# Turning y with a DMA transpose from the sixth pair of chunks on, in a fused gated-recurrence and MLP kernel

## The chip, the cores and the metric

The kernel runs on one core of one Trainium2 chip. Five engines run side by side, each with its own list of instructions: PE (TensorE, matrix products), ACT (ScalarE), DVE (VectorE), POOL (GpSimd) and SP (SyncE, which here only starts transfers). The metric is the device time of one execution in microseconds. Three runs of the kernel before gave 177.77, 177.81 and 180.62 us; the median is 177.81.

## The reference

First a recurrence with decay, for 4 sequences of 768 tokens, 8 heads of 48 dimensions; then an MLP with squared ReLU on every token:

```python
for t in range(S):                       # S = 768, state is D x D per head, D = 48
    state = alpha[:, :, t, :, None] * state + np.einsum('bhd,bhe->bhde', k[:, :, t], v[:, :, t])
    y[:, :, t] = np.einsum('bhd,bhde->bhe', q[:, :, t], state)
x = y.transpose(0, 2, 1, 3).reshape(3072, 384)
out = np.square(np.maximum(x @ w_in, 0)) @ w_out      # w_in 384 x 2048, w_out 2048 x 384
```

Inputs and output are float32; the products run in bfloat16 and sum in float32.

## The kernel before

**Tiling.** A chunk is 128 tokens and a pair is two chunks, 256 tokens of one sequence. There are 12 pairs (`g` from 0 to 11), three to a sequence; the state passes from chunk to chunk inside a sequence. The sixth pair is `g` = 5. One partition holds two neighbouring tokens (an even and an odd one), so that a tile of 128 partitions and 2 x 384 columns is a pair.

**Stages of a pair.**
- `loads`: four transfers of 384 KB on SP's queue (alpha, k, q, v), into one of four buffers RAW.
- `decay`: DVE and ACT turn alpha into running products, with a small product on PE (`sums`, L502 and L504; L541 and L546 in the first two pairs). k and q are scaled by them into QKS (L523, or L555).
- `turned`: QKS is transposed into QKT, with dimensions on partitions. The first three pairs do it on PE (L606, L574); from the fourth on (`TURN` = 3) one DMA transpose on SP's queue does it (L586, 16 blocks of 128x128, 512 KB).
- `scores`: q times k inside a chunk on PE (L634), masked by DVE into PMB (L644).
- `carry`: k times v on PE (L663); DVE and POOL make the next states of it in SBF (L681, L683).
- `mixed`: y = scores times v plus q times the state before (L702). It is computed turned, features on partitions and tokens along the columns: 48 products of 64 rows, 64 weights and 128 columns from PMB and VBF, and 24 (12 in the first pair of a sequence) from QKT and SBF. The last half of the 24 waits until the others have left PE, since it works crosswise on the same rows and banks. ACT copies the two results (L739) into XT, which is as the next stage reads it.
- `up`: eight units a pair on PE (L756, 12 products of 128x128 weights and 256 columns each); ACT takes the ReLU (L760), DVE the square (L762). Two PSUM banks, psH, hold the results in turn.
- `down`: for each chunk four parts on PE (L780, 4 products of 384 columns each), a copy by ACT (L787) and a store of 192 KB (L789). `last_down` (L800) does the last chunk in two halves.

`scores`, `carry` and `mixed` use the array as four tiles of 64x64; the others use it whole. The planner marks these operations with `form=64`.

**What sets the order.** `add` records every operation with what it reads and writes, an estimated length (`work`) and a due time (`at`, in chunks). `Program.order` plays the whole kernel through on those estimates, engine by engine: of the operations that are ready it takes the one with the earliest due time, keeps PE in one form where the due times allow it, and models SP's and POOL's transfers as queues. The order that results is written into the program; waits on semaphores are then placed where two engines meet (`plan`). The due times come from offsets by stage: EARLY for the first two pairs, MID for the third, OFF for the others (L811 to L813). `fill` puts products on zeros (`busy`, L769) into PE's idle times before the first `down`, to keep its clock up.

**Weights.** w_in and w_out come on POOL's queue in eight pieces of 786 KB (L446, L449), the first of them issued after alpha of the second pair has landed. The loads of the third pair wait for the sixth piece, `wout1` (`OPENS`). Loads on SP keep their order among themselves (`behind`).

Of the kernel before, what the change touches and what calls it, by code (L numbers as in the profile page):

```python
# [15 lines left out]
class Op:  # L16


    def __init__(self, n, eng, fn, work, at, dma=None, nbytes=0, rate=0.0):
# [7 lines left out]
        self.form = None  # L27


class Program:  # L30
# [4 lines left out]
    RESERVE, LATE = 200, 1200.0  # L35
    AHEAD = 4
    BEGIN = {"SP": 1200.0, "POOL": 2200.0}
    LANDING = {"SP": 900.0, "POOL": 1400.0}
    PAIR, ROWS, TURN = 320.0, 390.0, 135.0
    PACKET = {PAIR: 384.0, TURN: 256.0}  # L40
    LONG = 1792.0
    HOLD = 2500.0
    SWITCH, STICK = 95.0, 1.0

# [7 lines left out]
    def add(self, eng, fn, work, at, reads=(), writes=(), dma=None, nbytes=0, rate=0.0, behind=None, form=None,  # L52
            drain=None):
# [25 lines left out]
        op.form = form  # L79
# [3 lines left out]
    def order(self):  # L83
# [26 lines left out]
        def transfer(limit):  # L110

            while now[0] < limit:
# [20 lines left out]
                if queue[first][0][1] <= 1e-3:  # L133
                    op = queue[first].pop(0)[2]
                    op.landed = op.landed0 = end + self.LANDING[first]
                    if op.at > -2 and op.rate == self.PAIR:
                        op.landed += self.LATE
                    if first == "SP":
                        landed.append(op.landed0)
# [10 lines left out]
        form = None  # L150
        while left:
# [38 lines left out]
            if e == "PE":  # L190
                if op.form != form:
                    op.work += self.SWITCH
                form = op.form
            free[e] = t + op.work
# [21 lines left out]
        self.programs = programs  # L216

# [85 lines left out]
def bass_gla_recurrent__then__act_relu_squared_kernel(  # L303
# [31 lines left out]
    NS, NU, NAC, NRO = 5, 3, 3, 2  # L335
    NGT, NRR, NOS = 3, 4, 8
# [17 lines left out]
    XT = sb("xt", [128, KT, G * TW], BF16)  # L354
# [72 lines left out]
    WH = 4  # L427
    FIRST = 2
    TURN = 3
    SELF = 12  # L430


    RUNS = [(1, 3, 8)]
    OPENS = {2: 5}
    pieces = [(w, n) for w in ("in", "out") for n in range(WH)]
    last_weight, last_load = [None], [None]

    def weights(at, run):
        x0 = sum(r[2] for r in RUNS[:run])
        w0, j0, n0 = RUNS[run]  # L440
        for x in range(x0, x0 + n0):
            which, i = pieces[x]
            gate = raw(w0, j0) if x == x0 else []
            if which == "in":
                w = DFF // WH
                fn = lambda g, i=i, w=w: g.dma_start(WIN[:, :, i * w:(i + 1) * w], win_src[:, :, i * w:(i + 1) * w])  # L446
            else:
                w = FT // WH
                fn = lambda g, i=i, w=w: g.dma_start(WOUT[:, i * w:(i + 1) * w, :], wout_src[:, i * w:(i + 1) * w, :])  # L449
            last_weight[0] = add("POOL", fn, 770, at, reads=gate, writes=[("w" + which, i)], dma=f"w{which}{i}",  # L450
                                 nbytes=DM * DFF * 4 // WH, rate=(305.0, 305.0, 370.0, 370.0, 395.0)[min(x, 4)],
# [12 lines left out]
    def loads(g, at):  # L464
        b, t0, r = g // NW, (g % NW) * TW, g % NRAW
        for j, src in ((3, alpha), (0, k), (1, q), (2, v)):
            s = src[b, :, t0:t0 + TW, :].rearrange("h (p i) d -> p h (i d)", i=2)
            dst = RAW[:, r, j, :].rearrange("p (h e) -> p h e", h=H)
            gate = [("w" + pieces[OPENS[g]][0], pieces[OPENS[g]][1])] if g in OPENS and j == 3 else []
            cuts = (0, 1) if g == 0 and j == 3 else (None,)  # L470
            for X in cuts:
# [5 lines left out]
                                   nbytes=TW * HD * 4 // len(cuts), rate=pr.PAIR, behind=last_load[0])  # L477
# [9 lines left out]
    def decay(g, at):  # L487
# [19 lines left out]
        add("PE", sums, 265, at + 0.02, reads=lab + ["hinc"], writes=[key])  # L507
# [388 lines left out]
```

## Time and profile before

| | |
|---|---|
| median of 3 runs | 177.81 us |
| profiled execution, its own time | 177.77 us |
| its span, first to last instruction | 175.8 us |
| PE busy | 168.7 us (96%), 2648 products |
| DVE busy | 116.5 us (66%) |
| ACT busy | 116.2 us (66%) |
| SP's queue | 28.32 MB, 65.0% of the DMA engines' time |
| POOL's queue (weights) | 3.15 MB by its packets, 11.6% |

The span is 1.97 us shorter than the execution's own time. All times in this document are counted from the start of the span. PE is busy in nearly all of it, but some of that work is fill: 22 products on zeros, 7.5 us, all in the first 27 us. The granted clock of PE is 9 tenths or more in all 40 slices. A product's own duration in a row is its way through the array; products overlap, so that what one costs is the distance between two starts. The start times of the timeline rows are therefore subtracted from each other where a cost is wanted.

### The profile page before, as it was taken

What the parts mean: (1) busy time and instruction counts of PE and PEld (TensorE: products, weight loads), DVE (VectorE), ACT (ScalarE), POOL (GpSimd) and SP (SyncE); (2) the same over time, 40 slices, a digit from 0 to 9 for tenths busy, and PEclk for the clock granted to TensorE, in tenths of its full rate; (3) what the DMA queues carried; (4) which work ended last, traced back from release to release, by engine and by line L of the source; (5) the groups of instructions that cost most, each with busy time, mean ns of one, the idle gap of its engine ahead of it and who ended that gap; (6) DMA issues with size and microseconds to landing.
All of it is one profiled execution on the core that took longest, in us unless ns stands there. A gap on an engine that the chain in (4) does not pass through costs nothing.

```text
span 175.8 us, 6062 instructions
## 1 busy us (share of the span) xinstructions
PE 168.7 (96%) x2648; PEld 123.7 (70%) x2648; DVE 116.5 (66%) x251; ACT 116.2 (66%) x235; POOL 18.6 (11%) x35
## 2 busy tenths in 40 slices
PE   7889979999999999999999999999999999999994
PEld 2556658775677777777777776777777777767763
DVE  7895925589979597887965966946836733621410
ACT  4774555695885888879788869747546544645631
POOL 4089300001100201001002001001002000000000
PEclk9999999999999999999999999999999999999999
DMA  5999999999999999999999998901901701101112
GB/s 131 303 300 179 197 203 244 278 318 301 239 248 277 250 261 246 307 180 306 243 235 312 258 265 239 141 28 50 164 4 48 164 4 48 45 4 45 45 45 90
DMA packets 75993, 31.83 MB, mean 181 GB/s; under 512 B 69184, under 2 KB 75968, under 8 KB 75968
## 3 DMA queue, kind: packets, MB, share of 16 engines
q1 hardware_dynamic: 72256, 28.32, 65.0%
q0 software_dynamic: 3712, 3.15, 11.6%
q8 instruction: 20, 0.33, 0.7%
q14 instruction: 5, 0.04, 0.1%
HBM read 25.17 MB, written 4.72 MB: 170 GB/s over the span
## 4 chain that ended last, share of the span: by engine, by line
PE 87%; DVE 3%; ACT 3%; DMA 3%; issue 2%; SPq 1%
PE psH L756 35%; PE psO L780 34%; PE psG L702 8%; PE psG L634 4%; DMA raw<-in_q_dram 3%; DVE pm L644 2%; PE psG L663 2%; ACT xt L739 2%; PE psO L800 2%; PE psG L502 1%; DVE qks L555 1%; ACT rr L760 1%; SPq L474 1%; PE psG L574 1%; DVE ust L681 1%
## 5 line engine op out<-in xcount | busy, mean ns | idle before, releaser
L760 ACT ACTIVATE rr<-psH 128x512 bf16<-128x512 f32 x96 | 56.9, 599 | 35.5 <-PE psH L756 34.6
L756 PE MATMUL psH<-xt,win 128*128 128x256 bf16 x576 | 74.3, 273 | 0.5 <-ACT xt L739 0.4
L780 PE MATMUL psO<-wout,gt 128*128 128x384 bf16 x368 | 71.2, 326 | 0.0
L756 PEld LDWEIGHTS psH<-xt,win 128*128 128x128 bf16 x576 | 54.8, 98 | 13.9 <-ACT xt L739 0.8
L762 DVE TENSOR_TENSOR gt<-rr 128x512 bf16<-128x512 bf16 x96 | 39.8, 425 | 36.7 <-ACT rr L760 36.3
L780 PEld LDWEIGHTS psO<-wout,gt 128*128 128x128 bf16 x368 | 34.5, 98 | 17.2
L644 DVE TENSOR_TENSOR pm<-psG,mask 128x512 bf16<-128x512 f32 x48 | 30.9, 684 | 1.2 <-PE psG L634 1.2
L523 DVE TENSOR_TENSOR qks<-raw,asb 128x768 bf16<-128x768 f32 x20 | 18.4, 956 | 8.1 <-ACT asb L512 8.1
L683 POOL TENSOR_TENSOR sbf<-ust,acp 128x192 bf16<-128x192 f32 x16 | 8.8, 551 | 119.1 <-DVE ust L681 119.1
L739 ACT ACTIVATE xt<-psG 128x384 bf16<-128x384 f32 x24 | 12.6, 596 | 6.6 <-PE psG L702 6.6
L787 ACT ACTIVATE osb<-psO 128x384 f32<-128x384 f32 x23 | 11.4, 494 | 5.2 <-PE psO L780 4.8
L702 PEld LDWEIGHTS psG<-pm,vbf 64*64 64x64 bf16 x576 | 8.4, 107 | 3.7 <-issue 1.8
L702 PE MATMUL psG<-pm,vbf 64*64 64x128 bf16 x576 | 10.4, 218 | 0.6 <-DVE qks L555 0.3
L493 DVE TENSOR_TENSOR raw<-raw 128x384 f32<-128x384 f32 x20 | 10.6, 551 | 0.0
L512 ACT ACTIVATE asb<-psG 128x384 bf16<-128x384 f32 x20 | 9.9, 495 | 1.1 <-PE psG L504 0.8
L702 PE MATMUL psG<-qkt,sbf 64*64 64x128 bf16 x240 | 8.6, 220 | 1.0 <-issue 1.0
L634 PEld LDWEIGHTS psG<-qkt 64*64 64x64 bf16 x384 | 5.8, 106 | 4.3 <-issue 2.4
L634 PE MATMUL psG<-qkt 64*64 64x128 bf16 x384 | 8.1, 219 | 0.6 <-ACT qkt L617 0.4
L769 PE MATMUL psO<-warm 128*128 128x512 bf16 x22 | 7.5, 463 | 1.1 <-DVE warm L391 1.1
L485 ACT ACTIVATE vbf<-raw 128x768 bf16<-128x768 f32 x10 | 8.4, 841 | 0.0
L681 DVE TENSOR_TENSOR ust<-psG,sbf 128x192 f32<-128x192 f32 x15 | 5.3, 355 | 2.6 <-POOL sbf L683 1.9
L498 ACT ACTIVATE lab<-raw 128x384 bf16<-128x384 f32 x10 | 5.2, 520 | 2.2 <-DVE raw L493 2.2
(65 smaller groups left out, 99.5 us busy)
## 6 DMA issues: line engine op xcount, KB each, us to landing
raw<-in_k_dram SPq DMA_DIRECT2D x12, 384.0 KB, 5.0
raw<-in_q_dram SPq DMA_DIRECT2D x12, 384.0 KB, 5.6
raw<-in_v_dram SPq DMA_DIRECT2D x12, 384.0 KB, 5.4
out_dram<-osb SPq DMA_DIRECT2D x23, 192.0 KB, 2.0
raw<-in_alpha_dram SPq DMA_DIRECT2D x11, 384.0 KB, 4.5
win<-in_moe_w_in_dram POOLq DMA_DIRECT2D x4, 384.0 KB, 7.9
wout<-in_moe_w_out_dram POOLq DMA_DIRECT2D x4, 384.0 KB, 12.4
raw<-in_alpha_dram SPq DMA_DIRECT2D x2, 192.0 KB, 2.8
```

Source lines behind the costliest of these rows:

```text
L493: add("DVE", lambda e: e.tensor_tensor(dst, a0, a1, ALU.mult), 470, at_, reads=reads, writes=writes)
L512: add("ACT", lambda act, z=z: act.activation(ASB[a][:, z, 0, :], ps[:, 0:HD], AF.Exp, scale=2.0 * z - 1.0), 372, at + 0.04 + 0.02 * z, rea ...
L523: add("DVE", lambda dve, z=z, decays=decays: dve.tensor_tensor(QKS[x][:, z, :, :, 0:D], both(r, z), decays, ALU.mult), 870, at + 0.05 + 0. ...
L634: last = pe.matmul(banks[i, j // 2][0][64 * c:64 * c + 64, col:col + 128].rearrange("p (a b) -> p a b", a=2), QKT[t][64 * i:64 * i + 64, 0 ...
L644: add("DVE", lambda dve, i=i, X=X, ps=ps: dve.tensor_tensor(PMB[m][:, i, 2 * X:2 * X + 2].rearrange("p j n s -> p j (n s)"), ps[:].rearran ...
L702: last = pe.matmul(o, lhsT, rhs, start=(c, n % 2) not in begun, stop=True, skip_group_check=True)
L739: add("ACT", lambda act, ps=ps, base=base: act.activation(XT[:, :, base:base + C].rearrange("f k (p i) -> f k i p", i=2), ps[:, 0:HD].rear ...
L756: last = pe.matmul(ps[:, f * TW:(f + 1) * TW], WIN[:, kt, fj * 128:(fj + 1) * 128], XT[:, kt, g * TW:(g + 1) * TW], start=(kt == 0), stop= ...
L760: add("ACT", lambda act: act.activation(RR[r][:], ps[:], AF.Relu), 480, at, reads=[key], writes=[key, ("rr", r)])
L762: add("DVE", lambda dve: dve.tensor_tensor(gt[:, 2 * u:2 * u + 2, :], rr, rr, ALU.mult), 340, at, reads=[("rr", r)], writes=[("gt", g % NG ...
L780: last = pe.matmul(ps[:, 0:DM], GT[g % NGT][:, fj, tt * 128:(tt + 1) * 128], WOUT[:, fj, :], start=(fj == 0), stop=(fj == FT - 1))
L787: add("ACT", lambda act: act.activation(OSB[o][:], ps[:, 0:DM], AF.Copy), 372, at, reads=[key], writes=[key, ("osb", o)])
```

## The change

From the sixth pair on (`BACK` = 5), `mixed_back` takes the place of `mixed`. It computes y with tokens on partitions: 64 products of 48 columns from PMB and VBF, and 32 (16 in the first pair of a sequence) of 48 columns from QKT and SBF, with the operands changed over. ACT copies the two results into a new buffer YB, and a DMA transpose on SP's queue (6 blocks of 128x128, 192 KB) writes XT. The tokens then stand in XT as the partitions held them, all even ones ahead of all odd ones, and `store` writes the rows of the output accordingly. XT becomes a ring of six pairs.

The rest of the change is in the order. OFF now holds from the sixth pair on; the fourth and fifth pair have offsets of their own (NEXT), and EARLY and MID have new numbers. In `mixed`, the products that need the state become an operation of their own. The planner has new constants; it counts PE's instructions, and adds a delay where it expects the next 256 of them to arrive late (`take`). Fill products have 128 columns and not 512. w_in comes in five pieces (256, 256, 512, 512 and 512 columns) and w_out in four, w_out issued after v of the second pair has landed; the loads of the third pair wait for the first piece of w_out.

The core of the diff (new calls of `size=` and renamings of reads are left out):

```diff
@@ class Program
-    RESERVE, LATE = 200, 1200.0
+    RESERVE, LATE = 0, 1200.0
+    LATE_BACK = 1000.0
-    BEGIN = {"SP": 1200.0, "POOL": 2200.0}
+    BEGIN = {"SP": 1200.0, "POOL": 2700.0}
-    PAIR, ROWS, TURN = 320.0, 390.0, 135.0
-    PACKET = {PAIR: 384.0, TURN: 256.0}
+    PAIR, ROWS, TURN, EARLY = 325.0, 390.0, 135.0, 200.0
+    PACKET = {PAIR: 120.0, TURN: 256.0}
+    BLOCK, AHEAD_OF_ALL, FETCH, CALM, BUSY_UNTIL = 256, 37, 5200.0, 1800.0, 36000.0
+    FILL, SHARE = 58.0, 0.75
...
+    def take(self, used, size, t, work, there):
+        late = 0.0
+        block = used // self.BLOCK
+        for b in range(block + 1, (used + size) // self.BLOCK + 1):
+            at = t + late + work * (b * self.BLOCK - used) / size
+            late += max(0.0, there.get(b, 0.0) - at)
+            there[b + 1] = max(at, there.get(b, 0.0)) + self.FETCH - (self.CALM if at > self.BUSY_UNTIL else 0.0)
+        return used + size, there, late
...
-    XT = sb("xt", [128, KT, G * TW], BF16)
+    XT = sb("xt", [128, 2 * NX, KT, C], BF16)
+    YB = sb("yb", [128, 2, HD], BF16, NY)
...
-    RUNS = [(1, 3, 8)]
+    RUNS = [(1, 3, 5), (1, 2, 4)]
     OPENS = {2: 5}
-    pieces = [(w, n) for w in ("in", "out") for n in range(WH)]
+    CUTS = {"in": (0, 2, 4, 8, 12, 16), "out": (0, 4, 8, 12, 16)}
+    pieces = [(w, a, b) for w in ("in", "out") for a, b in zip(CUTS[w], CUTS[w][1:])]
...
-            return before(pe, 0, last)
-        reads = [("qkt", t, 1, 0), ("qkt", t, 1, 1), ("vbf", vb)] + [("pm", m, i, jj) for i in range(2) for jj in range(2)]
-        reads += [("sbf", (2 * g + c) % NS) for c in chunks]
-        first = add("PE", mm, 640 + 80 * len(chunks), at, reads=reads, writes=[b[1] for b in banks], form=64)
+            return last
+        add("PE", mm, 640, at, reads=[("vbf", vb)] + [("pm", m, i, X) for i in range(2) for X in range(2)],
+            writes=[b[1] for b in banks], form=64, size=96)
+        first = add("PE", lambda pe: before(pe, 0), 80 * len(chunks), at + 0.004, reads=reads, writes=keys, form=64,
+                    size=12 * len(chunks))
...
+    def mixed_back(g, at):
+        t, m, vb, b_ = g % NQT, g % NPM, g % NV, g % NY
+        banks = [bank() for c in range(2)]
+        chunks = [1] if g % NW == 0 else [0, 1]
+        def before(pe, swap):
+            for j in range(NP):
+                for i in range(2):
+                    c = i ^ swap
+                    for n in range(2):
+                        if c in chunks:
+                            h = 2 * j + i
+                            last = pe.matmul(banks[c][0][64 * n:64 * n + 64, D * h:D * h + D],
+                                             QKT[t][64 * i:64 * i + 64, 1, n, j, 64 * c:64 * c + 64],
+                                             SBF[(2 * g + c) % NS][64 * i:64 * i + 64, D + PAD * j:2 * D + PAD * j],
+                                             start=False, stop=True, skip_group_check=True)
+            return last
+        def mm(pe):
+            for h in range(H):
+                for i in range(2):
+                    for c in range(2):
+                        for n in range(2):
+                            last = pe.matmul(banks[c][0][64 * n:64 * n + 64, D * h:D * h + D],
+                                             PMB[m][64 * c:64 * c + 64, h % 2, h // 2, i, 64 * n:64 * n + 64],
+                                             VBF[vb][64 * c:64 * c + 64, i, h, 0:D],
+                                             start=(h, i) == (0, 0), stop=True, skip_group_check=True)
+            return last
...
+            add("ACT", lambda act, c=c, ps=ps: act.activation(YB[b_][:, c, :], ps[:, 0:HD], AF.Copy), 400, at + 0.02 * c + 0.01,
+                reads=[key], writes=[key, ("yb", b_, c)])
+        dst, src = XT[:, 2 * (g % NX):2 * (g % NX) + 2].rearrange("f c k t -> f (c k) t"), YB[b_][:].rearrange("p c f -> p (c f)")
+        add("SP", lambda sp: sp.dma_start_transpose(dst, src), 600, at + 0.04, reads=[("yb", b_, c) for c in range(2)],
+            writes=[("xt", g % NX, c) for c in range(2)], dma="back", nbytes=128 * 2 * HD * 2, rate=pr.TURN)
+    def store(o, n, cols=slice(None)):
+        rows, tile = out[n * C:(n + 1) * C, cols], OSB[o][:, 0:DM if cols == slice(None) else cols.stop - cols.start]
+        if n // 2 >= BACK:
+            rows = rows.rearrange("(p i) d -> i p d", i=2)
+        return rows, tile
...
-    OFF = dict(decay=-5.14, turned=-4.136, scores0=-2.842, scores1=-2.061, carry=-3.412, mixed=-1.443, up=-1.226)
-    EARLY = dict(decay=-6.102, turned=-5.566, scores0=-5.314, scores1=-4.089, carry=-5.284, mixed=-3.871, up=-2.03)
-    MID = dict(decay=-5.605, turned=-4.806, scores0=-3.382, scores1=-3.16, carry=-4.451, mixed=-1.982, up=-1.395)
+    OFF = dict(decay=-5.8, turned=-5.3, scores0=-3.3, scores1=-3, carry=-4.1, mixed=-2.35, up=-0.888)
+    NEXT = dict(decay=-4.387, turned=-4.027, scores0=-1.833, scores1=-1.83, carry=-2.149, mixed=-0.838, up=-0.271)
+    EARLY = dict(decay=-6.086, turned=-5.597, scores0=-4.501, scores1=-4.348, carry=-4.083, mixed=-3.655, up=-0.598)
+    MID = dict(decay=-5.434, turned=-4.483, scores0=-2.98, scores1=-2.954, carry=-3.545, mixed=-0.628, up=-0.591)
...
-        o = EARLY if g < FIRST else MID if g < TURN else OFF
+        o = EARLY if g < FIRST else MID if g < TURN else NEXT if g < BACK else OFF
```

## The prediction

> **What bounds the kernel now.** I read the chain that ended last, then busy time by stage, then single stretches of PE's timeline.
>
> ```profile
> PE 87%; DVE 3%; ACT 3%; DMA 3%; issue 2%; SPq 1%
> ```
> ```profile
> 0.00:27.36 27.36, 23.13 (x401) 15.08 (x402) 19.36 (x54) 15.54 (x32) 11.74 (x22) 1.00 1.09 218
> 27.36:47.00 19.64, 19.26 (x286) 13.48 (x283) 15.27 (x30) 14.04 (x31) 0.51 (x1) 1.00 1.10 291
> 47.00:104.20 57.20, 57.19 (x929) 43.35 (x929) 47.05 (x96) 46.68 (x96) 3.81 (x7) 1.00 1.08 256
> 104.20:173.20 69.00, 69.00 (x1040) 51.74 (x1039) 34.83 (x73) 39.57 (x77) 2.54 (x5) 1.00 0.32 77
> ```
>
> The second fence cuts the span at 27.36 (the first `down`, L780), 47.00, 104.20 and 173.20 (the last product). After the stretch and its length come busy us of PE, PEld, DVE, ACT and POOL, the granted clock, the DMA share and GB/s. From 47 us on PE has no gap: 57.19 of 57.20, then 69.00 of 69.00. So the time is 27.36 of start-up, 145.84 in which PE's work and a few waits count, 2.6 of last copy and store, and 1.97 outside the span: 177.77, the profiled execution, 0.04 under the median of the runs. The DMA engines are full up to 104 us.
>
> **Part 1: `mixed` itself.**
>
> ```profile
> 117.08 0.86 PE L702 MATMUL psG<-pm,vbf 64*64 64x128 bf16 x48
> 117.77 0.34 PE L702 MATMUL psG<-qkt,sbf 64*64 64x128 bf16 x12
> 117.94 0.42 PE L663 MATMUL psG<-vbf,qks 64*64 64x48 bf16 x32
> 118.19 0.37 PE L702 MATMUL psG<-qkt,sbf 64*64 64x128 bf16 x12
> 118.49 0.82 PE L780 MATMUL psO<-wout,gt 128*128 128x384 bf16 x4
> ```
> ```profile
> 122.77 0.76 PE psH L756 x6
> ...
> 124.18 0.65 PE psH L756 x6
> ```
>
> Subtract starts (first column): 48 products of 128 columns take 0.69 us, 14.5 ns each; 12 take 0.17, 14 each; 32 of 48 columns (`carry`) take 0.25, 7.9 each. `mixed_back` consists of products of this last shape, over the same four tiles in the same turn, so 7.9 is the row I take. Behind the first `down` the kernel before has 684 products of L702 (480 at 14.5, 204 at 14: 9.8 us). The order after has 204 of them, of three pairs (144 and 60: 2.9), and 640 of `mixed_back` (5.1). That is 1.8 us less.
>
> From it goes the change of form. The chain (second fence) gives six products of L756 behind the scores 0.76 us, otherwise 0.65: 0.11 to leave the 64x64 form. Entering costs 0.09, by the same subtraction (0.75 for the six ahead of L702). PE changes into the form 22 times behind the first `down` before, 27 times after, as the new due times put `down` parts between the halves of `mixed` and of `scores` in pairs 3 to 5. Five times 0.20 is 1.0. **Part 1 is -0.8.** Bounds: if columns alone counted, 48 would take 5.4 ns, -1.6 more; if 48 columns took 14.5 as 128 do, +4.2.
>
> The Trainium skill, "TensorEngine Tiling (Array Packing)", section Instruction Overhead, says that a matmul has some 60 cycles of overhead, so that few columns cost as much as 60 would. That speaks against small columns: 60/128 of 14.5 is an estimated 6.8 ns in place of 5.4; the row, at 7.9, is above it. By the page part 1 would be -1.5.
>
> **Part 2: the start-up.**
>
> ```profile
> 9.12 0.42 PE L634 MATMUL psG<-qkt 64*64 64x128 bf16 x16
> 9.63 0.44 PE L663 MATMUL psH<-vbf,qks 64*64 64x48 bf16 x32
> 10.34 0.42 PE L634 MATMUL psG<-qkt 64*64 64x128 bf16 x16 [0.27 <-DVE pm L644]
> 13.12 0.87 PE L702 MATMUL psG<-pm,vbf 64*64 64x128 bf16 x48 [0.31 <-DVE qks L555]
> ...
> 20.92 0.86 PE L702 MATMUL psG<-pm,vbf 64*64 64x128 bf16 x48 [0.29 <-DVE ust L681]
> 21.62 0.22 PE L702 MATMUL psG<-qkt,sbf 64*64 64x128 bf16 x2
> 22.85 0.35 PE L702 MATMUL psG<-qkt,sbf 64*64 64x128 bf16 x10 [1.01 <-issue]
> ```
> ```profile
> PEld psG L702 <- ACT acp L559: 0.8, 1, 0.8
> ```
> ```profile
> q8 instruction: 20, 0.33, 0.7%
> ```
>
> Before, `carry` of the first pair stands between the halves of its `scores` and takes 0.71 us for a work of 0.25; the first `mixed` then waits for a copy out of a bank that the second pair's decay sums share with it (second fence; L559 ends at 13.06). After, both halves of `scores` come first and the sums have other banks: `mixed` needs only four masks of L644, from 9.59 at 0.60 each on DVE, 12.0, and 0.1 to get to PE. It starts a microsecond earlier, near 12.1.
>
> The third fence is the instruction queue: 20 packets and 0.33 MB, 16.4 KB each. Two start times in the trace, 12.12 and 20.52, follow PE's 103rd and 225th product (10.5 and 17.1 us) by 1.6 and 3.4. The line at 22.85 is the stall that belongs to it: PE waits 1.0 us for nothing but "issue", 1.4 after the second packet ends, 5.7 after the 225th product. A packet so brings some 122 products with their weight loads, and is asked for when PE enters the one before. The order after has more, smaller fill products: 78 products, not 44, ahead of the first `scores`. It reaches the 103rd at 9.4 and the 225th, in the first `mixed`, at 13.2. The packet is there 3.9 us after the first crossing (if it begins 1.6 later) or 5.7: at 13.3 or 15.1, a stall of 0.1 to 1.9; I take 0.8, near the first, since the queues there carry the same loads as at 12.12. The copies of L739 (1.05 for both) then let `up` begin at 15.4, where it was 17.14; the half-sized first piece of w_in has landed by then (a whole one took 2.1 us behind 14.30). The second pair's scores follow together at 16.5, their four masks end at 19.2, its `mixed` starts at 19.4 and not 20.92, and wants the next packet there, which is due between 18 and 20.0: 0.3. From there PE has 48 + 24 products of `mixed`, six units of `up` at 0.66, three changes of form and 0.35 of fill: 6.4 us in all. First `down` at 26.1, **part 2 is -1.2**. Bounds: -1.9 without a stall, +0.5 where the second packet comes as late as it did at 22.85 and the first stall is whole. The weights are no bar: wout0 landed at 24.59, and the same bytes lie ahead of it.
>
> **Part 3: between 27 and 50 us.**
>
> ```profile
> 47.01 1.16 PE L756 MATMUL psH<-xt,win 128*128 128x256 bf16 x9 [0.39 <-ACT xt L739]
> ```
>
> This is the one wait behind the first `down` in the kernel before: `up` of the third pair's y, 0.57 by the starts (four products of L780 from 45.80 on need 0.65). After, a `down` part of 0.65 and a change of form stand between the halves of this `mixed`, the copies of L739 come that much later, and `carry` of the fourth pair behind it needs QKS of L523, ended at 45.10. PE idles 1.0 instead of 0.6. Then four units of `up` stand in a row: with two banks, a unit (0.66), the way to ACT (0.2), its copy (0.48 between starts) and the way back (0.16) make 1.5 for two, 0.1 to 0.2 lost on each of three. **Part 3 is +0.9**, bounds +0.3 and +1.5.
>
> **Part 4: the new transposes.** The rows do not show this transpose, only its neighbours of 16 blocks.
>
> ```profile
> DMA to landing us min/median/max: 4.2/5.4/6.9
> ```
>
> Queued among loads of 1.2 us each, one of L586 takes 3.2 between the landings around it. Six blocks are 1.2 by size, and issue to landing is between 1.9 (a store of the same 192 KB in quiet) and 6.9. From the end of `mixed_back` to the first `up` that reads XT the order has 42 products of L756, 16 of L780, one decay sum and the next scores: 8.1 us of PE (6.5 for the last pair). In it lie 0.2 to ACT, up to 0.6 until ACT is free, two copies (0.37 between starts, 0.49 the last), 0.2 to SP: 1.7. The transpose then may take 6.4. In quiet 4.7 holds; I cost it at **nothing**, hidden by other pairs' `up` and `down`. Behind it on SP stand stores and loads; loads of the last pairs landed 20 us ahead of use (alpha of the last at 105.01, its sum on PE at 132.7), and only those of pairs 6 to 8 are near. Pairs 6 on need their loads up to 6 us earlier; alpha and k of the sixth are moved ahead of a 3.2 us transpose and two stores, so that they come as much earlier. Upper end: the rival below. ACT's copies get shorter and ACT is not full.
>
> **Sum.** 177.77 - 0.8 - 1.2 + 0.9 = **176.7 us**, the span 174.7.
>
> **Rivals.**
> - *The transposes come late (slower).* Where DMA is full, SP hands over a transpose in up to 3.9 us and takes nothing else; the first one for y stands right behind the seventh pair's L586. With 6.9 it misses its 6.4 by 0.5, with the other ahead of it by up to 4.4. Sixth pair 2.5, next three 0.5 each: 4.0, 180.7; twice that if scores miss L586 too. It decides from 6.4 us between issue and landing. For it: DMA share 1.08 up to 104 us. Against: size.
> - *The start-up gives nothing.* Both stalls whole: +0.5 in place of -1.2, 178.4.
> - *The instruction packets come in time.* Part 2 is -1.9, and 176.0. The Trainium skill, "Runtime: NRT & Kernel Launch", section Instruction fetch mechanics, says that crossing a 16 KiB boundary is mostly hidden. The 1.01 us above disagrees for one of 20; no other is seen behind 27 us.
> - *48 columns cost what 128 do*, and the change does not shorten `mixed`: +4.2, 180.9. Against it: L663 loads weights of the same size and runs at 7.9.
>
> **How the numbers follow.** Forecast 0.50 (175.7 to 177.8 by itself), late transposes 0.17, nothing from the start-up 0.16, packets in time 0.12, no shorter products 0.05. The likeliest gives 176.7. The range, 175.0 to 180.8, leaves out half of the two cases that end at 180.7 or above and the low end of the others. 2% is 3.6 us, about what a measurement of this kernel can tell from no change. Faster than 174.2 needs the low bounds of parts 1 and 2 together: 0.06. Slower than 181.4 is a good half of the late transposes and of the last rival: 0.12. Within 2%: 0.82.
>
> **What would show it.** Part 1: 64 products of `mixed_back` in 0.5 us between starts. Part 2: first `down` near 26.1, one "issue" wait under 1 us near 13. Part 3: PE idle some 1.6 between 44 and 50. Part 4: no wait of `up` on the transpose. Wrong if PE waits for XT or QKT in every pair, or if an "issue" wait recurs where 96 and 32 small products stand together, about one packet's worth.

## The result, and the profile after

The changed kernel takes 193.92 us (median of 4 runs, 193.46 to 196.18), the kernel before beside it 177.79 (4 runs). The ratio is 1.0945, 95% interval [1.0835, 1.1055]: 9 per cent slower, where 176.7 was forecast. Ratios, here and below, are formed without disturbed executions, so one can differ a little from the quotient of the medians beside it.

The profiled execution took 193.46 us, its span 191.5 (before 177.77 and 175.8). Cut at the first `down` and at the start of the last product, the two spans compare like this:

| stretch | before | after | difference |
|---|---|---|---|
| start to the first `down` | 27.36 | 26.18 | -1.2 |
| first `down` to the last product | 145.74 | 154.72 | +9.0 |
| last product to the end | 2.66 | 10.58 | +7.9 |

In this execution the start came out as forecast. The loss lies in the other two stretches. First the shares of the chain that ended last, of the profile's page after (before: PE 87%, DMA 3%, SPq 1%):

```profile
PE 75%; DMA 10%; SPq 6%; issue 2%; ACT 2%
```

Transfers and the sequencer that issues them now carry 16 per cent of the span. The windows by stage, after (start:end, length, then busy us of PE, PEld, DVE, ACT, POOL, the granted clock, the DMA share, GB/s), say where:

```profile
0.00:26.34 26.34, 23.68 (x453) 17.93 (x454) 19.63 (x54) 15.95 (x32) 12.55 (x23) 1.00 1.11 221
...
99.00:116.00 17.00, 16.69 (x379) 12.41 (x377) 10.49 (x22) 12.07 (x26) 0.51 (x1) 1.00 0.94 207
116.00:126.00 10.00, 6.09 (x76) 3.99 (x74) 5.71 (x12) 5.26 (x13) 0.51 (x1) 0.94 0.70 160
126.00:134.00 8.00, 8.00 (x144) 5.13 (x143) 3.12 (x7) 3.10 (x6) 0.40 (x1) 0.65 0.72 100
134.00:181.20 47.20, 47.15 (x615) 35.12 (x613) 19.30 (x41) 24.67 (x47) 1.13 (x3) 1.00 0.28 59
181.20:191.50 10.30, 0.00 (x0) 0.00 (x0) 0.00 (x0) 0.31 (x1) 0.00 (x0) 0.75 0.12 45
```

Three rows are new. Between 116 and 126 PE stands still for 3.9 us. For the next 8 us it is busy throughout, but at a mean granted clock of 0.65: 8.00 x 0.35 = 2.8 us lost with no gap to be seen. The 0.65 is a mean over two values: from 124.84 to 131.67 us the granted clock is 0.50, behind that 1.00. Behind the last product 10.30 us pass in which PE, PEld and DVE do nothing and ACT makes one copy; at 45 GB/s, stores are what is left. The same stretch before:

```profile
173.20:175.80 2.60, 0.14 (x2) 0.00 (x0) 0.00 (x0) 0.33 (x1) 0.00 (x0) 1.00 0.24 76
```

The wait has a name in PE's list of waits, after:

```profile
PE psH L843 <- DMA xt<-yb: 3.9, 1, 3.9
PE psG L735 <- issue: 1.5, 2, 0.8
...
PE psG L792 <- issue: 0.8, 1, 0.8
```

`up` (L843) waits once for a transposed y. That looks like the rival "the transposes come late", but the chain between 99 and 131 us, after (start, length, what; SPq is SP's sequencer while it issues), tells what came ahead:

```profile
102.96 0.70 SPq L879
...
104.18 8.50 DMA raw<-in_v_dram
...
115.42 1.95 SPq L507
...
117.41 3.40 SPq L507
...
120.85 4.80 DMA xt<-yb
...
125.79 1.44 PE psH L843 x6
```

L879 is a store. The load of v behind it (L507) takes 8.5 us; before, the median of that load was 5.4. ACT, which waits for this v before its next copies, hands on the ninth pair's y only at 116.5. SP is then held 1.95 and 3.40 us in issuing two more loads, and only at 120.85 takes the transpose, which itself lands in 4.80, a time that part 4 allowed (6.4). So the transpose is not slow, it is issued late, and behind a store. The list of transfers, after (count, KB each, median us from issue to landing), points to the stores too:

```profile
out_dram<-osb SPq DMA_DIRECT2D x23, 192.0 KB
...
qkt<-qks SPq DMA_TRANSPOSE x9, 7.0
xt<-yb SPq DMA_TRANSPOSE x7, 4.1
```

The first row carries no landing time any more. Before, it did:

```profile
out_dram<-osb SPq DMA_DIRECT2D x23, 192.0 KB, 2.0
```

The trace's small packets explain it. A transfer ends with packets of 4 bytes that report its completion. The last four stores of the kernel before leave 64 of them, 16 each. The last four after leave 8: two each. The data of the last two half stores (256 packets of 768 bytes) ran from 186.47 to 190.71, 2.1 us for a half store and so 4.2 for a whole one. A store from the sixth pair on uses 2 of the 16 DMA engines.

The cause is the row pattern that the change wrote into `store`: "(p i) d -> i p d" makes 2 x 64 rows of 384 out of 128 rows. The Trainium skill, "DMA: Bandwidth & Descriptors", section "Why a DMA increments its semaphore by 16 and not by 1", says that the outermost number of each pattern decides: the largest number up to 16 that divides it on both sides is the number of engines. By it 128 gives 16 and 2 gives 2; the packets agree with both.

### The profile page after: what moved, and what is told of

Same layout as the page of the kernel before. It is cut to its first block, busy times and chain, and to the rows that moved or that the text cites. A ratio compares the mean times of both kernels' runs of the same rounds, so it can differ in the third digit from the quotient of the medians.

```text
span 191.5 us, 6506 instructions
## 1 busy us (share of the span) xinstructions
PE 172.6 (90%) x2860; PEld 125.8 (66%) x2860; DVE 118.0 (62%) x251; ACT 116.0 (61%) x235; POOL 19.5 (10%) x36
## 4 chain that ended last, share of the span: by engine, by line
PE 75%; DMA 10%; SPq 6%; issue 2%; ACT 2%
PE psH L843 31%; PE psO L870 29%; SPq L507 5%; DMA raw<-in_v_dram 4%; PE psG L735 3%; PE psG L667 3%; DMA raw<-in_alpha_dram 3%; DMA xt<-yb 3%; PE psG L803 2%; PE psG L696 2%; PE psO L890 1%; PE psG L792 1%; PE psO L858 1%; PE psG L535 1%; PE psG L639 1%
## 5 line engine op out<-in xcount | busy, mean ns | idle before, releaser
L843 PE MATMUL psH<-xt,win 128*128 128x256 bf16 x576 | 78.1, 277 | 4.4 <-DMA xt<-yb 3.9
L870 PE MATMUL psO<-wout,gt 128*128 128x384 bf16 x368 | 74.0, 331 | 0.0
L843 PEld LDWEIGHTS psH<-xt,win 128*128 128x128 bf16 x576 | 55.2, 99 | 20.5 <-issue 4.6
L851 DVE TENSOR_TENSOR gt<-rr 128x512 bf16<-128x512 bf16 x96 | 40.7, 431 | 43.7 <-ACT rr L849 43.1
L858 PE MATMUL psO<-warm 128*128 128x128 bf16 (+1 forms) x74 | 8.9, 261 | 1.0 <-DVE warm L420 1.0
L818 ACT ACTIVATE yb<-psG 128x384 bf16<-128x384 f32 x14 | 6.3, 489 | 3.2 <-PE psG L792 3.1
L774 ACT ACTIVATE xt<-psG 128x384 bf16<-128x384 f32 x10 | 5.5, 600 | 4.2 <-PE psG L735 4.2
L858 PEld LDWEIGHTS psO<-warm 128*128 128x128 bf16 x74 | 5.2, 102 | 2.8 <-issue 1.7
L526 DVE TENSOR_TENSOR raw<-raw,ro 128x384 f32<-128x384 f32 x10 | 5.5, 552 | 1.7 <-DMA raw<-in_q_dram 0.9
L696 PE MATMUL psG<-vbf,qks 64*64 64x48 bf16 x288 | 5.2, 188 | 0.8 <-ACT xt L774 0.8
```

The costliest lines, as they stand in the source:

```text
L526: add("DVE", lambda e: e.tensor_tensor(dst, a0, a1, ALU.mult), 470, at_, reads=reads, writes=writes)
L843: last = pe.matmul(ps[:, f * TW:(f + 1) * TW].rearrange("p (c t) -> p c t", c=2), WIN[:, kt, fj * 128:(fj + 1) * 128], XT[:, 2 * (g % NX): ...
L851: add("DVE", lambda dve: dve.tensor_tensor(gt[:, 2 * u:2 * u + 2, :], rr, rr, ALU.mult), 340, at, reads=[("rr", r)], writes=[("gt", g % NG ...
L858: last = pe.matmul(psO[i % NPO][:, 0:128 * wide].rearrange("p (a b) -> p a b", a=wide), WARM[:], bass.AP(tensor=WARM, offset=0, ap=[[128, ...
L870: last = pe.matmul(ps[:, 0:DM], GT[g % NGT][:, fj, tt * 128:(tt + 1) * 128], WOUT[:, fj, :], start=(fj == 0), stop=(fj == FT - 1))
```

## The experiments

The theory is that the stores on two engines cost most of the 16 us, by late loads, a wait, the low clock behind it and a long tail. The rivals are the transposes themselves, `mixed_back` with its many small products, and the new due times.

### The store's pattern taken out, and put in alone

In the kernel after:

```diff
 def store(o, n, cols=slice(None)):
-    if n // 2 >= BACK:
-        rows = rows.rearrange("(p i) d -> i p d", i=2)
```

> The kernel after, with one thing undone: the rows of pairs six to twelve are stored as one block of 128 rows again, in place of 2 x 64. (The tokens then stand in the output with all even ones of a chunk ahead of all odd ones; that reordering is left out, no other work.) Theory A, narrow store: a store whose row pattern leads with a 2 runs on 2 of the 16 DMA engines; its 14 stores fill those two, hold up every load and transpose that shares them, and run on after the last product. Then the wait of up on XT (4.1 us), the low clock behind it (some 3.0), a wait of 0.5 at 113 and 7.7 of the tail go: 191.5 - 15.2 = 176.3 span, 178.3 us (177.5 to 179). Theory B, late transposes: y's transposes come late because the engines are full and SP hands transfers over in order, whatever the form of the store: only the tail shortens, 185 to 187 us.

Measured: 181.45 us, ratio 1.0155 [1.0109, 1.0201]. The wait for XT, the low clock and the long tail are gone. The last two windows of this run:

```profile
104.20:177.60 73.40, 72.38 (x1089) 54.10 (x1086) 37.53 (x78) 44.38 (x86) 2.03 (x4) 1.00 0.51 114
177.60:180.20 2.60, 0.21 (x3) 0.00 (x0) 0.00 (x0) 0.33 (x1) 0.00 (x0) 1.00 0.24 76
```

The kernel after was 16.1 us over the kernel before beside it, this run is 2.8 over its own. So 13.3 of the 16.1 us belong to the pattern, with the same transposes in the same places. But 2.8 stay, where theory A had none.

And in the kernel before:

```diff
+    def rows_of(n, cols=slice(None)):
+        rows = out[n * C:(n + 1) * C, cols]
+        return rows.rearrange("(p i) d -> i p d", i=2) if n // 2 >= 5 else rows
-            add("SP", lambda sp: sp.dma_start(out[n * C:(n + 1) * C, :], OSB[o][:]), 600, at,
+            add("SP", lambda sp: sp.dma_start(rows_of(n), OSB[o][:]), 600, at,
```

> The kernel before, with the store pattern of after alone: rows of pairs six to twelve written as 2 x 64. (y is not reordered here, so that tokens are written to swapped rows; the work is the same.) Theory A: the last four stores take 4.2, 4.2, 2.1 and 2.1 us on two engines, the tail behind the last product is 8 to 11 us and not 2.6, so at least 185 us; more if loads or transposes come so late that PE waits. Theory B: the store's form costs nothing, 177.8 us.

Measured: 192.58 us, ratio 1.0688 [1.0587, 1.0788]. The pattern alone makes the kernel before nearly as slow as the kernel after, 7 per cent against 9. The profiled execution took 193.47 us, the longest of the four. PE's longest wait in it, by its list of waits, is another one:

```profile
PE psG L634 <- ACT acp L518: 3.2, 1, 3.2
```

`scores` waits for work that starts from an alpha, which was issued at 106.80, right behind such a store, and landed 7.9 us later. There are no transposes of y here. Which load comes late depends on the order; that one does, depends on the stores. The end is the same: 10.6 us from the last product.

The same run with another leading number:

```diff
-        return rows.rearrange("(p i) d -> i p d", i=2) if n // 2 >= 5 else rows
+        return rows.rearrange("(p i) d -> i p d", i=8) if n // 2 >= 5 else rows
```

> The kernel before with the stores from the sixth pair on written in another row pattern, as 8 x 16 rows of 1536 bytes in place of 128 (in the run with 2 x 64 rows the time was 192.6); the rows of the output stand in another order, all else is as before. Theory A (the leading number of the pattern sets how many DMA engines carry a store: 2 with 2 x 64, 8 with 8 x 16): a store takes some 4.2 us by 2/8, near 1.1, and is hidden; 177.5 to 180, and the small completion packets of a store come 8 at a time. Theory B (a scattered order of rows is slow in itself, whatever the leading number): 188 to 194.

Measured: 180.63 us median of 5 (178.88 to 185.05), ratio 1.0078 [1.0035, 1.0121]. The rows are as scattered as with 2 x 64, but the last five stores leave 40 completion packets, 8 each. Theory A holds: the leading number counts, not the scatter. Of the 6.9 per cent 0.8 stay.

The last run of this group is the kernel after with two transfers for each of these stores:

```diff
+        rows = rows.rearrange("(p i) d -> i p d", i=2)
+        return [(rows[i], tile[64 * i:64 * i + 64]) for i in range(2)]
...
-            add("SP", lambda sp: sp.dma_start(*store(o, n)), 600, at,
+            add("SP", lambda sp: send(sp, o, n), 600, at, parts=len(store(o, n)),
```

> The kernel after, each store of the 2 x 64 form sent as two transfers of 64 rows each, to the same rows. Theory A: each of the two again runs on 16 engines, so that the gain of the plain store comes back with the right order of rows: 178.3 to 179.3 us, up to 1 us for 14 more transfers to start. Theory B: as the kernel after less its tail, 185 to 187 us.

Measured: 181.37 us, ratio 1.015 [1.0106, 1.0194], the same as with the plain store. Two transfers of 64 rows keep the tokens of the output in order and have 16 engines each. Again 2.7 us over the kernel before stay. The split is not free at the end: from the start of the last product to the end of the span 3.61 us pass, where the run with the plain store takes 2.66, as the kernel before does.

### What the other 2.7 us are

The rows of the first of these runs show candidates. PE's weight-load waits, plain store in the kernel after:

```profile
PEld psG L735 <- issue: 3.2, 6, 1.2
PEld psG L792 <- issue: 2.8, 3, 1.4
```

L792 is the second half of `mixed_back`. Twice, at 75 and 116 us, 16 of its products take 1.56 and 1.47 us, by the starts, where the same 16 take 0.13 and 0.24 to 0.26 in other pairs, 1.4 and 1.2 more. PE waits for nothing but "issue" there. That is what part 2 had read at 22.85 as late instruction packets. Two runs take away what could bring it on. The first has wide fill products in the kernel after, with two transfers a store:

```diff
-    def busy(pe, n, wide=1):
+    def busy(pe, n, wide=4):
-    FILL, SHARE = 58.0, 0.75
+    FILL, SHARE = 217.0, 0.75
```

> The kernel after with each store of a back pair as two transfers of 64 rows, and the fill products ahead of the first down part 512 columns wide again (the planner's count for them as it was before). Theory A (what is left of the loss, 2.7 us over the kernel before, is late instruction packets, which more and smaller fill products bring on): the start-up stalls of 1.2 and 1.4 us shrink, 179.0 to 180.5 us. Theory B (the number of fill products does not matter, the due times or the transposes cost it): 181.0 to 182.0, as with narrow fill.

Measured: 182.35 us (181.13 to 184.28), ratio 1.0219 [1.016, 1.0278]. Fewer fill products bring nothing. The stall in `mixed_back` stays (1.5 us at 74.7), a wait of 0.8 for XT appears. Theory A falls as far as the fill goes.

The second is the kernel after without `mixed_back`; the due times are kept:

```diff
-    BACK = 5
+    BACK = 12
...
-        o = EARLY if g < FIRST else MID if g < TURN else NEXT if g < BACK else OFF
+        o = EARLY if g < FIRST else MID if g < TURN else NEXT if g < 5 else OFF
```

> The kernel after without mixed_back: mixed in all pairs, no transposes for y, plain stores, all due times and the start-up as after. Theory A (packet stalls inside mixed_back, 1.4 and 1.2 us, eat what its short products save): 181.0 to 182.5, the products 1.8 us longer and the two stalls mostly gone. Theory B (mixed_back saves its 1.8 us whole): 183 to 184. Theory C (the transposes and their waits cost the 2.7 us): 178 to 179.5.

Measured: 180.62 us, ratio 1.016 [1.0108, 1.0211], the same as with `mixed_back` and a plain store (1.0155). `mixed_back` and its transposes are worth nothing in this order: neither the 1.8 us of their products come through (theory B), nor do they cost the 2.7 (theory C). The time lies just under theory A's 181.0, and only one of the two stalls is gone: there is one of 1.35 us in the sixth pair here too, now in `carry`. It is bound to the place, not to the kind of product.

That leaves the question whether the stall is the packets at all. One run brings such a stall about in the kernel before:

```diff
-            for y in range(2 * KT):
+            for y in [y for again in range(3 if g == 8 else 1) for y in range(2 * KT)]:
+                if y == 0:
+                    begun.clear()
```

> The kernel before with the 48 products of 128 columns in the ninth pair's mixed issued three times over, the last time counting: 96 products more in one place, the output the same. They cost 1.4 us by the 14.5 ns of one. Theory A (a burst of more than some 122 products outruns the instruction packets, which come about 4.7 us after PE enters the packet before): an issue wait of 0.8 to 1.8 us inside or right behind the burst, and +2.2 to +3.2 us in all, 180.4 to 181.4. Theory B (no such limit): +1.4, 179.6, and no issue wait.

Measured: 181.97 us, beside 179.3 of the kernel before in this comparison, ratio 1.0229 [1.0061, 1.0396]. The 2.7 us lie in theory A's 2.2 to 3.2. The interval is wide, but the timeline of PE shows the stall itself:

```profile
118.15 2.20 PE L702 MATMUL psG<-pm,vbf 64*64 64x128 bf16 x144
120.19 0.34 PE L702 MATMUL psG<-qkt,sbf 64*64 64x128 bf16 x12
120.35 0.42 PE L663 MATMUL psG<-vbf,qks 64*64 64x48 bf16 x32
120.60 0.24 PE L702 MATMUL psG<-qkt,sbf 64*64 64x128 bf16 x2
122.14 0.35 PE L702 MATMUL psG<-qkt,sbf 64*64 64x128 bf16 x10 [1.29 <-issue]
```

By the starts, 144 products take 2.03 us, 14.1 ns each as always. Then PE stops between two products of one operation, at 120.6, and goes on 1.4 us after the end of an instruction packet that ran from 119.82 to 120.77. The kernel with two transfers a store shows the same figure in its sixth pair, in PE's timeline:

```profile
74.33 0.70 PE L805 MATMUL psG<-vbf,pm 64*64 64x48 bf16 x64
74.85 0.22 PE L794 MATMUL psG<-sbf,qkt 64*64 64x48 bf16 x5
76.59 0.28 PE L794 MATMUL psG<-sbf,qkt 64*64 64x48 bf16 x11 [1.52 <-issue]
```

There the packet ran from 74.13 to 75.06, and PE goes on 1.5 us behind it.

The traces of all runs settle it. Counted from the first product of a trace, "issue" stalls of 0.4 us and more stand at four places only: after 221, 347, 1240 and 2004 or 2005 products. Which products stand there differs from run to run. With wide fill the places are the same in the count, though 55 fill products fewer lie ahead of them. The distances are 126, 7 x 127.6 and 6 x 127.5, so that a packet brings some 127 products with their weight loads. In all 24 of these stalls PE goes on 1.2 to 1.5 us after a packet has ended.

The Trainium skill, "Runtime: NRT & Kernel Launch", section Instruction fetch mechanics, calls the cost of a block boundary mostly hidden. Here it is hidden at most of them. Behind the first `down` none to two of them in a run cost 0.8 to 1.5 us, and the 127 products ahead of those had passed in 1.8 to 3.4 us; some stretches as short did not stall.

### One part of the order at a time

The kernel after without `mixed_back`, with wide fill and with the old due times from the third pair on:

```diff
-    BACK = 5
+    BACK = 12
...
-    OFF = dict(decay=-5.8, turned=-5.3, scores0=-3.3, scores1=-3, carry=-4.1, mixed=-2.35, up=-0.888)
-    NEXT = dict(decay=-4.387, turned=-4.027, scores0=-1.833, scores1=-1.83, carry=-2.149, mixed=-0.838, up=-0.271)
+    OFF = dict(decay=-5.14, turned=-4.136, scores0=-2.842, scores1=-2.061, carry=-3.412, mixed=-1.443, up=-1.226)
+    NEXT = OFF
...
-    MID = dict(decay=-5.434, turned=-4.483, scores0=-2.98, scores1=-2.954, carry=-3.545, mixed=-0.628, up=-0.591)
+    MID = dict(decay=-5.605, turned=-4.806, scores0=-3.382, scores1=-3.16, carry=-4.451, mixed=-1.982, up=-1.395)
```

> The kernel after without mixed_back, with wide fill, and with the due times of the kernel before from the third pair on: only the start-up (first two pairs' due times, five pieces of w_in, the separate sums bank) and the planner's constants are new. Theory A (the start-up is worth some 1.2 us, as the first down part showed): 176.5 to 178.0. Theory B (the start-up gain is given back by the stalls that follow it): 178.3 to 179.5.

Measured: 182.17 us, ratio 1.0246 [1.0207, 1.0285]. Both theories miss. The first `down` is early as hoped, at 26.43, but behind it PE loses more than it does with the new due times: 1.00 at 45 us, 0.70 and 0.69 at 50 and 51, 1.1 in three waits up to 97. In this run the early start only moves the waits to the third pair and its neighbours; it was not tested apart from the planner's new constants.

The opposite combination is the kernel after, with two transfers a store, in which the start-up, the first five pairs and the planner's constants are as they were before. Of its diff, the order's part:

```diff
-    RUNS = [(1, 3, 5), (1, 2, 4)]
+    RUNS = [(1, 3, 8)]
...
-    CUTS = {"in": (0, 2, 4, 8, 12, 16), "out": (0, 4, 8, 12, 16)}
+    CUTS = {"in": (0, 4, 8, 12, 16), "out": (0, 4, 8, 12, 16)}
...
-    NEXT = dict(decay=-4.387, turned=-4.027, scores0=-1.833, scores1=-1.83, carry=-2.149, mixed=-0.838, up=-0.271)
-    EARLY = dict(decay=-6.086, turned=-5.597, scores0=-4.501, scores1=-4.348, carry=-4.083, mixed=-3.655, up=-0.598)
+    NEXT = dict(decay=-5.14, turned=-4.136, scores0=-2.842, scores1=-2.061, carry=-3.412, mixed=-1.443, up=-1.226)
+    EARLY = dict(decay=-6.102, turned=-5.566, scores0=-5.314, scores1=-4.089, carry=-5.284, mixed=-3.871, up=-2.03)
```

> The turned y alone: mixed_back, its transposes and its due times from the sixth pair on as in the kernel after, each of its stores as two transfers of 64 rows; the start-up, the pieces of the weights, the due times of the first five pairs, the fill and the planner's constants as in the kernel before. Theory A (the packet stalls and waits that stay come from the new start-up and from the new places of the third to fifth pair): 176.5 to 178, as mixed_back then gives its 1.8 us, less the form changes. Theory B (they belong to mixed_back, whose short products stand together): 179 to 181.

Measured: 180.32 us median of 10, beside 179.3 of the kernel before, ratio 1.0085 [1.0028, 1.0143]. Behind 27 us no "issue" wait of 0.5 us or more is left, as theory A had it, but the gain it promised isn't there. The median lies in theory B's 179 to 181, which were meant beside some 178 for the kernel before; in this comparison that was itself at 179.3. By the starts, `mixed` and `mixed_back` behind the first `down` take 9.9 us where `mixed` took 11.2, a gain of 1.3; `up` takes 1.1 more, `carry` 1.2 and `scores` 0.5, in 29 changes of form instead of 22 and in waits near 46 and 50 us. In the profiled execution this makes 1.0 us more behind the first `down`. Another 0.95 is the longer end of the split stores, 3.62 us from the start of the last product as against 2.66; the start is 0.3 shorter.

In the same kernel, the old due times for the later pairs as well:

```diff
-    OFF = dict(decay=-5.8, turned=-5.3, scores0=-3.3, scores1=-3, carry=-4.1, mixed=-2.35, up=-0.888)
+    OFF = dict(decay=-5.14, turned=-4.136, scores0=-2.842, scores1=-2.061, carry=-3.412, mixed=-1.9, up=-1.226)
```

> As the run before it, but the stages from the sixth pair on keep the due times of the kernel before too, only mixed_back is due half a chunk earlier than mixed was. Theory A: 176.5 to 178, and no issue wait over 1 us behind 27 us, since the small products of a pair stay apart. Theory B (mixed_back's products stall wherever they stand): 179 to 181. Theory C (transposes come late, since less time is left for them): waits of up on XT of 0.5 us and more, 179 to 182.

Measured: 182.1 us, ratio 1.0202 [1.0064, 1.0339]. Theory C: with less time ahead of `up` the transposes do come late. PE's list of waits:

```profile
PE psH L852 <- ACT rr L858: 1.9, 3, 1.4
...
PE psH L852 <- DMA xt<-yb: 1.0, 1, 1.0
PE psG L669 <- DMA qkt<-qks: 0.9, 1, 0.9
```

L858, in the row with ACT, is the ordinary copy of `up`, which takes 0.6. Its longest wait, 1.38 us up to 122.83, goes back to a load as well: ACT stood idle for 1.85 us until a v had landed at 120.67 and made three other copies before this one. The median is a little over theory C's range.

### Two side questions

Could the store have been left as it was, and the order of tokens put right where XT is read?

```diff
-                    XT[:, 2 * (g % NX):2 * (g % NX) + 2, kt, :]
+                    XT[:, 2 * (g % NX):2 * (g % NX) + 2, kt, :].rearrange("f c (i p) -> f c p i", i=2)
```

> The kernel after, with the reordering moved to PE: up reads XT of pairs six to twelve through a view that takes even and odd tokens in turn (step of 64 elements inside 128), and stores are one block of 128 rows. Theory A: as the plain store, 178.3 us, if a stepped moving operand costs PE nothing; if PE reads it at half the rate, products of L843 in seven pairs (336 of 109 ns) cost up to 37 us more. Theory B: 185 us or more.

Measured: 224.63 us, ratio 1.2592. The group of `up` in this run, and below it that of the run with the plain store, by the groups of instructions (busy us, mean ns of one):

```profile
L845 PE MATMUL psH<-xt,win 128*128 128x256 bf16 x576 | 121.3, 350 | 2.5 <-DMA win<-in_moe_w_in_dram 1.5
```

```profile
L841 PE MATMUL psH<-xt,win 128*128 128x256 bf16 x576 | 76.6, 273 | 0.6 <-ACT rr L847 0.4
```

By the starts, a product whose moving operand jumps to and fro costs 243 ns and not 109. 336 products changed, 336 x 134 = 45 us; 43 were measured.

And is the low clock the work of the stores, or of the pause? In the kernel before, one copy of no use on ACT, ahead of the tenth pair's second copy of y, makes PE pause:

```diff
+            def copy(act, ps=ps, base=base, idle=(g, c) == (9, 1)):
+                if idle:
+                    act.activation(XT[:, :, 0:6 * TW], WIN[:, :, 0:6 * TW], AF.Copy)
```

> The kernel before with one idle copy of 4608 columns by ACT (about 4.4 us by the 0.37 us that 384 columns take) ahead of the tenth pair's second copy of y, so that PE stands still once, some 3 to 4 us, near 120 us. The output is the same. Theory A (an idle gap of this length is followed by some us of low granted clock): 184 to 187, and the clock row falls to 0.5 to 0.7 for 5 to 8 us behind the gap. Theory B (the low clock behind the wait of the kernel after has another cause, as its stores): 181 to 182.5, clock 1.0 throughout.

Measured: 184.19 us, ratio 1.0337 [1.0302, 1.0372]. The windows behind the pause (PE waited 3.42 us up to 138.63):

```profile
138.63:142.00 3.37, 3.37 (x18) 2.09 (x18) 2.16 (x3) 2.41 (x6) 0.00 (x0) 0.60 0.16 58
142.00:147.00 5.00, 5.00 (x68) 3.88 (x68) 4.00 (x8) 2.29 (x5) 0.00 (x0) 1.00 0.60 122
```

A pause of 3.4 us with no slow store near is followed by a mean clock of 0.60, which costs 3.37 x 0.40 = 1.3 us. (The clock is 0.50 from 137.92 to 141.34.) Theory A, though for 3.4 us and not for 5 to 8. The Trainium skill, "TensorE: Matmul & The Clock Gate", section "Part 1: The HAM clock gate", puts the limit for a pause at some 3.4 us. The pauses of 3.42 here and 3.91 in the kernel after reach it, but other traces of this case do not agree, and the measurement decides. Shorter pauses were followed by 3.4 us at a clock of 0.50 too: 1.62 and 3.22 us in the run with 2 x 64 in the kernel before, 2.09 in the run with two transfers a store, and 2.04 in this run, near 6 us. In no profile did a pause of 1.54 us or less have this effect.

Pause and clock make 4.7 of the 6.0 us. In the profiled execution the first `down` came at 29.49, which is 2.1 later than in the profile of before: the pause near 6 us and the half clock from 8.22 to 11.63 lie ahead of it.

## Why the prediction was wrong

**The step that failed** is the end of part 4 with the unchanged tail: "Behind it on SP stand stores and loads", and 2.6 us of last copy and store taken over. The diff had a new row pattern in `store`; the working mentions the store only as a thing that stands in a queue, and its cost was never worked out. The sum so took a store at the speed of before (1.9 us to landing in quiet). It occupies two engines for 4.2 us, and there are 14 of them in the seven pairs. That is worth 13.3 us by the run without it and some 12.3 by the ratio of the run with it alone. The rival of late transposes had the right victim and the wrong cause: its condition, more than 6.4 us between issue and landing, was not met (4.80); the transpose was issued late.

**Part 1** (-0.8): the price of a product held. 64 of them took 0.53 us between starts in the kernel after, 8.2 ns each against 7.9 forecast; the rival of 48 columns at the price of 128 falls, and so does the 5.4 of columns alone. The changes of form are 27 against 22, as counted. What was missed are the stalls: this part was summed with no instruction packet behind 27 us, though the text named the sign, "an 'issue' wait recurs where 96 and 32 small products stand together". It recurs there, 0.77 us in the kernel after, 0.9 to 1.5 in its variants. With it `mixed_back` is worth nothing: the run without it has the same ratio.

**Part 2** (-1.2): met in the profile of the kernel after, in part by luck. The first `down` stands at 26.18, forecast near 26.1, and the first stall is the one forecast, 0.8 near 13. PE's timeline, after:

```profile
12.57 0.27 PE L735 MATMUL psG<-qkt,sbf 64*64 64x128 bf16 x3
13.65 0.27 PE L735 MATMUL psG<-qkt,sbf 64*64 64x128 bf16 x3 [0.81 <-issue]
...
19.21 0.35 PE L735 MATMUL psG<-pm,vbf 64*64 64x128 bf16 x9
20.22 0.75 PE L735 MATMUL psG<-pm,vbf 64*64 64x128 bf16 x39 [0.66 <-issue]
```

The second is 0.66 instead of 0.3. The last step of the sum holds a slip: the items that it lists add up to 5.9 us and not to 6.4, by which the first `down` would have been forecast at 25.6. A packet brings some 127 products, not 122.

Over executions the start scatters by more than the gain. The five profiles with this start-up and its narrow fill have the first `down` at 26.18, 27.95, 28.47, 27.63 and 26.48; those of the kernel before and its variants have it at 27.36, 29.16, 29.49, 27.73 and 27.56. The means differ by 0.9. But 28.47, 29.16 and 29.49 had 3.4 us of half clock ahead of it; without these three the means are 27.1 and 27.5, and the gain is 0.5. The direction is as forecast, the size is not shown, and 26.18 is the earliest of five. No figure of the start should have been read from one execution.

**Part 3** (+0.9): right. PE's timeline, after:

```profile
46.04 0.44 PE L696 MATMUL psG<-vbf,qks 64*64 64x48 bf16 x32 [0.78 <-ACT xt L774]
```

By the starts the idle time is 0.98 there and 0.42 over the four units of `up` behind it, 1.4 between 44 and 50; "some 1.6" was forecast.

**Part 4**: the transposes as such cost nothing or little, as forecast. They land in 4.1 us at the median. (The terms on their way add up to 1.9 us and not 1.7, which changes nothing here.) Without the slow stores PE's list has no wait for XT in the runs with the plain store and with two transfers, and one of 0.8 us with wide fill. That hangs on the long lead of the new due times: with less of it they are late.

Without the store the sum would have been 176.7 and the run without it gave 181.45, beside 178.64 of the kernel before: 2.8 more, not 1.1 less. In that execution the difference of 4.4 in the span is made of 0.6 of start, 2.6 of two stalls, 1.0 at 47 and 50 us as in part 3, and 0.3 for all that is left: the shorter products against changes of form and the waits that come with them. So apart from the store one missing term is the packets, 0.8 to 2.6 us by the execution. Their share of the 2.7 in the medians isn't settled: in the order without stalls behind 27 us the loss is still 1.5 [0.5, 2.6] by its ratio. In that run's profile 0.95 of it is the end of the split stores, which the plain store doesn't have.

## What to carry to other kernels

When a diff changes the pattern of a transfer, cost the transfer anew, even if its bytes and its place stay: read the outermost number of the pattern on both sides first, and split a transfer rather than give it a leading 2. Look at completion packets and at a missing landing time to see how many engines carried it. When small products replace fewer larger ones, look at how many pass in one stretch and not only at the ns of one: here no 127 of them that took over 3.5 us stalled behind the first `down`.

## What the runs showed that had not been expected

- A store of 192 KB as 2 x 64 rows runs on 2 DMA engines in 4.2 us; loads queued behind it take 7.9 to 8.5 us where their median was 5.4. As 8 x 16 rows it runs on 8.
- A pause of PE costs more than itself: after 1.62 to 3.42 us the granted clock was 0.50 for 3.4 us, after 3.91 us for 6.8.
- A burst of short products outruns its own instructions: with 190 in 2.5 us PE stopped for 1.3 us. Such stalls stood at the same four places in the count of products.
- A moving operand that steps through its 256 columns in pairs from two places costs 243 ns a product instead of 109. Here the two places are 64 columns apart.
- Two transfers of 64 rows gave the time of one of 128, ratios of 1.015 and 1.0155, but an end that is 0.95 us longer.
